# Strassen products for the first dense layer of the last stage, and an earlier place for the transposes of q and k

## The chip, the cores and the metric

The kernel runs on one core of one Trainium2 chip. The metric is the device time of one execution in microseconds (us): lower is better. The time before is the median of three runs.

## The reference, cut to what matters

```python
# chunked attention: 4 batches, 8 heads, 576 positions in chunks of 64, head size 64
attn = softmax(q_c @ k_c.T / 8)            # within each chunk
x    = attn @ v_c                          # -> 2304 tokens x 512
# 8 experts on every token, weights P from a Sinkhorn iteration over x @ w_gate
out  = sum_e P[:, e] * (relu(x @ w1[e]) @ w2[e])      # 512 -> 1024 -> 512
# last stage, on the experts' output x (2304 x 512)
h    = x @ w_in                            # 512 -> 1024
solu = h * exp(h - max(h)) / (sum(exp(h - max(h))) + 1e-9)
ln   = (solu - mean(solu)) / sqrt(var(solu) + 1e-6) * g_ln
out  = ln @ w_out                          # 1024 -> 512
```

## The kernel before, in words

**Precision.** Each large product is three matmuls: an operand is split into a high part (a copy on ScalarE, ACT) and a low part (source minus high, one subtraction on VectorE, DVE, or GpSimd, POOL). The function `split` does both; its subtraction is on DVE unless POOL is named. PASSES3 gives high*high, high*low, low*high.

**Stages.** The attention stage takes one tile of 128 tokens per step in the loop `for s in range(NT + 6)` (NT is 18, L1118). A step works on several tiles: exponentials of tile s-3, values (`attn_pv`, L277) of s-6, transposes of probabilities (`attn_pt`, L262) of s-5, scores (`attn_qk`, L217) of s-2, and at its end `attn_t(s)` (L199): the transposes of q (even s) or k (odd s) for a pair of tiles, evacuated from PSUM by ACT (L204) and DVE (L206). Scores of tile t need q and k of pair t//2, so for even t the k of the step just before. Side work (splits of the experts' weights and of x) goes to ACT and POOL in each step. The experts follow in 96 units (NM); already there the seven Strassen products of PRODUCTS are used for w1 (L653) and in pairs of units for w2 (`l2s`, L847). During the units the weights of the last stage are turned into two float32 parts on DVE, ACT and POOL, one small step at a time (`prep`, `mlp_steps`), and kept in DRAM.

**Last stage, per tile t of 128 tokens.** `mlp_x` loads x. `mlp_a` splits it (ACT and DVE). `mlp_b` (L1005) makes h: 24 matmuls of 512 columns into two PSUM banks; then the row maximum `nm` (L1019, DVE) and the exponential (L1020, ACT). `mlp_n` is the norm: the product un = h*ex (L1025, DVE), sums and statistics, one power on POOL (L1036), and the scaling of un (L1038). `mlp_c` (L1050) transposes un on PE and splits it (ACT, DVE). `mlp_d` (L1062) is the second layer, 24 matmuls of 512 columns, and stores the result. In the loop at L1294 a step s issues: `mlp_a(s+1)`, `mlp_b(s)`, `mlp_c(s-1)`, `mlp_n(s)`, `mlp_d(s-2)`.

**Passage.** After the last unit the last pair of units still has 14 products `l2s(last, k)`, k = 0 to 13, each with a DVE addition into the accumulator; the first tile's `mlp_b(0)` stands after k = 7. Then `l2s_sums` makes seven additions on DVE, one in each of the steps s = 3 to 9. The weights of the first layer arrive in eight tiles of 512 KB (`load_in`, tag "six", 15 buffers): one is loaded when a buffer is spare and seven as the x tiles of the last unit come free.

**Order.** The program runs in the order in which it is written (`manual_schedule`): each engine, and SP's DMA queue, works through its instructions in that order and stops at the first whose inputs or buffers aren't ready. PSUM tiles: four single banks ("r") and two double banks ("d").

Of the kernel before, what the change touches and what calls it, by code (L numbers as in the profile page):

```python
# [44 lines left out]
def chunk_attention_sinkhorn_moe_solu_kernel(  # L45
# [855 lines left out]
    raw64 = {}  # L901

    def load_mlp(n):
        i, j = divmod(n, 8)
# [6 lines left out]

    def mlp_steps(n):
        i, j = divmod(n, 8)
# [4 lines left out]
        def one():  # L918
            s["lo"], s["hi"] = raw64[n][:, :, 0], raw64[n][:, :, 1]
            s["b"] = two([P, 512], U32, f"wb{n}")  # L920
            ts(out=s["b"], in0=s["hi"], scalar1=3, scalar2=0x3FFFFFF8,
               op0=ALU.logical_shift_left, op1=ALU.bitwise_and)
# [32 lines left out]
        def store():  # L955
            for s_ in range(2):
                nc.sync.dma_start(
                    out=kept[i, s_][:, j * 512:(j + 1) * 512], in_=s["p"][s_].bitcast(F32)
                )

        return [one, two_, three, round_, rounded, size, flush_, parts, store]
# [3 lines left out]
    def load_in(kk, s_):  # L965
        t = six([P, F], F32R, f"mi{kk}_{s_}")
        nc.sync.dma_start(out=t.bitcast(F32), in_=kept[0, s_][:, kk * F:(kk + 1) * F])
        m_in[kk, s_] = t

    def load_out(n0, n1):  # L970
        for n in range(n0, n1):
            f, s_ = divmod(n, 2)
            if n % 3 == 0:
# [3 lines left out]
                out=t[:, n % 3].bitcast(F32), in_=kept[1, s_][:, f * DM:(f + 1) * DM]  # L977
# [16 lines left out]
    def mlp_a(t):  # L994
        x = xa.pop(t)
        xm[t] = [wtile([P, KD, P], F32R, f"xm{t}_{i}") for i in range(2)]
        split(xm[t][0], xm[t][1], x)

    def mlp_b(t):
        x = xm.pop(t)  # L1000
        ph = bank2(f"mh{t}")
        for n in range(2):
            for kk in range(KD):
                for i, (a, c) in enumerate(PASSES3):
                    nc.tensor.matmul(  # L1005
                        ph[:, n * 512:(n + 1) * 512],
                        x[a][:, kk, :],
                        m_in[kk, c][:, n * 512:(n + 1) * 512],
                        start=(kk == 0 and i == 0),
                        stop=(kk == KD - 1 and i == 2),  # L1010
                    )
# [64 lines left out]
    with tc.manual_schedule():  # L1076
# [41 lines left out]
        for s in range(NT + 6):  # L1118
# [33 lines left out]
            if s < NT:  # L1152
# [48 lines left out]
        for n in range(NM):  # L1201
# [30 lines left out]
            if n == NM - 1:  # L1232
                for t in range(3):
                    mlp_x(t)
            apart = n < 4
            parts = [(j, d, i) for d in (0, 2) for j in range(2) for i in range(2)]
            for i in range(7):
# [9 lines left out]
                if n == NM - 1:  # L1247
                    load_in(*divmod(i, 2))
# [90 lines left out]
```

## Time and profile before

| what | value |
|---|---|
| median of 3 runs | 1763.87 us (1761.92 to 1766.05) |
| profiled execution | 1770.89 us, its span 1769.1 us |
| busy share of the span | PE 99%, DVE 77%, POOL 62%, ACT 35% |
| attention stage | 0 to about 107 us |
| experts | about 107 to 1535 us |
| passage and last stage | 1534.7 us to the end |

Busy time of PE is the time in which a matmul is in flight; because matmuls overlap, the distance between the starts of groups tells more than their durations. A row names the line of the kernel, the engine, the operation, the tile written and the tiles read.

### The profile page before, as it was taken

The page shows a single profiled execution, that of the slowest core. Times are in us where ns is not written, and L with a number is a line of the kernel's source. Part 1 is how long each engine was busy: PE and PEld are TensorE (multiplying, and loading weights), DVE is VectorE, ACT ScalarE, POOL GpSimd, SP SyncE. Part 2 cuts the span into 40 slices and gives each one's busy share as a digit, 9 for nine tenths or more (in the row PEclk, how much of TensorE's full clock was granted, in tenths as well). Part 3 has the DMA queues.
Part 4 walks back from the last instruction along what each step waited for, and adds up shares of the span by engine and source line. Part 5 has one row for each costly group of instructions (what it writes and reads, how often), then busy time and mean ns, then how long its engine had stood idle before and what let it go on. Part 6 is the DMA issues. An engine that isn't in the chain of part 4 may idle for free. (4 is left out here: it accounts for less than half of the span.)

```text
span 1769.1 us, 32047 instructions
## 1 busy us (share of the span) xinstructions
PE 1744.6 (99%) x10809; PEld 1690.9 (96%) x10809; DVE 1364.3 (77%) x2249; ACT 627.2 (35%) x1424; POOL 1094.3 (62%) x1203
## 2 busy tenths in 40 slices
PE   8999999999999999999999999999999999999999
PEld 7899999999999999999999999999999999988887
DVE  5868888889987778787777688878777777776664
ACT  5843444444444223333322222232323222222222
POOL 2767988888887367778777766666666565400000
PEclk8999999999999999999999999999999999999999
DMA  9667899999898999989989999888888888931210
GB/s 221 175 221 261 297 316 331 324 344 325 317 332 322 342 340 339 332 293 357 313 295 343 337 329 369 302 284 281 283 264 281 276 276 253 311 110 49 66 49 30
DMA packets 299203, 481.45 MB, mean 272 GB/s; under 512 B 47248, under 2 KB 99616, under 8 KB 299040
## 3 DMA queue, kind: packets, MB, share of 16 engines
q1 hardware_dynamic: 298320, 475.47, 78.9%
q10 hardware_dynamic: 720, 3.93, 0.5%
q8 instruction: 87, 1.43, 0.3%
q14 instruction: 76, 0.62, 0.1%
HBM read 332.94 MB, written 146.35 MB: 271 GB/s over the span
## 5 line engine op out<-in xcount | busy, mean ns | idle before, releaser
L673 POOL TENSOR_TENSOR ho_T<-hT,ho_T 128x384 fp32r<-128x384 f32 x252 | 275.6, 1095 | 195.7 <-ACT ho_T L672 178.1
L796 PE MATMUL y<-h,w_A 128*128 128x384 f32 x1536 | 303.6, 335 | 0.5 <-DVE acc L823 0.5
L796 PEld LDWEIGHTS y<-h,w_A 128*128 128x128 f32 x1536 | 269.2, 188 | 1.3 <-ACT w_S L599 1.1
L672 ACT ACTIVATE ho_B<-hp 128x384 fp32r<-128x384 f32 x192 | 101.0, 526 | 416.7 <-DVE hp L706 400.2
L847 PE MATMUL y<-ho_T,wl_S 128*128 128x384 f32 x1152 | 231.4, 335 | 2.1 <-DMA wl_S<-wk 2.0
L152 POOL TENSOR_TENSOR w_A<-raw,w_A 128x256 fp32r<-128x256 f32 x224 | 173.1, 786 | 82.3 <-ACT w_A L151 77.9
L867 DVE TENSOR_TENSOR acc<-y,acc 128x768 f32<-128x768 f32 (+1 forms) x217 | 199.9, 923 | 24.3 <-PE y L847 24.0
L751 DVE TENSOR_TENSOR t<-Y,s 128x384 f32<-128x384 f32 x192 | 106.1, 553 | 136.8 <-PE Y L653 97.9
L847 PEld LDWEIGHTS y<-ho_T,wl_S 128*128 128x128 f32 x1152 | 202.7, 188 | 3.6 <-issue 2.6
L681 POOL TENSOR_TENSOR hT<-hp,hp 128x384 f32<-128x384 f32 x126 | 133.6, 1081 | 98.7 <-DVE hp L706 88.2
L672 ACT ACTIVATE ho_T<-hT 128x384 fp32r<-128x384 f32 x256 | 131.6, 516 | 125.2 <-POOL hT L681 120.5
L653 PE MATMUL X<-x_B,wl_A 128*128 128x384 f32 x768 | 154.6, 335 | 0.0
L653 PE MATMUL Y<-x_T,wl_S 128*128 128x384 f32 x768 | 154.1, 335 | 0.4 <-DVE t L751 0.3
L847 PE MATMUL y<-ho_B,wl_A 128*128 128x384 f32 x768 | 153.6, 334 | 0.3 <-DMA wl_A<-wk 0.3
L673 DVE TENSOR_TENSOR ho_B<-hp,ho_B 128x384 fp32r<-128x384 f32 x192 | 143.5, 747 | 3.9 <-ACT ho_B L672 3.3
L681 POOL TENSOR_TENSOR hT<-hp,hT 128x384 f32<-128x384 f32 x126 | 143.5, 1139 | 0.0
L1036 POOL TENSOR_TENSOR r<-r,mhalf 128x1 f32<-128x1 f32 x18 | 9.9, 550 | 208.8 <-DVE r L1033 208.8
L653 PEld LDWEIGHTS Y<-x_T,wl_S 128*128 128x128 f32 x768 | 134.7, 188 | 1.3 <-DVE t L751 1.3
L653 PEld LDWEIGHTS X<-x_B,wl_A 128*128 128x128 f32 x768 | 135.8, 189 | 0.0
L847 PEld LDWEIGHTS y<-ho_B,wl_A 128*128 128x128 f32 x768 | 134.7, 188 | 1.0 <-issue 1.0
L823 DVE TENSOR_TENSOR acc<-y,acc 128x768 f32<-128x768 f32 (+1 forms) x132 | 118.9, 901 | 5.0 <-PE y L796 4.5
L152 POOL TENSOR_TENSOR w_S<-ws,w_S 128x256 fp32r<-128x256 f32 x128 | 103.0, 822 | 6.3 <-ACT w_S L151 6.3
(169 smaller groups left out, 3463.1 us busy)
## 6 DMA issues: line engine op xcount, KB each, us to landing
wl_S<-wk SPq DMA_DIRECT2D x512, 256.0 KB, 4.8
wl_A<-wk SPq DMA_DIRECT2D x384, 256.0 KB, 4.7
wk<-w_S SPq DMA_DIRECT2D x256, 256.0 KB, 3.7
wk<-w_A SPq DMA_DIRECT2D x192, 256.0 KB, 3.4
raw<-in_moe_w_dram SPq DMA_DIRECT2D x71, 512.0 KB, 6.0
sh<-spread SPq DMA_DIRECT2D x64, 192.0 KB, 5.6
kept<-wp SPq DMA_DIRECT2D x32, 256.0 KB, 4.4
xk_T<-x_T SPq DMA_DIRECT2D x8, 768.0 KB, 4.3
```

What stands on the lines that cost most here:

```text
L152: (eng or nc.vector).tensor_tensor(out=lo, in0=src, in1=hi.bitcast(F32), op=ALU.subtract)
L653: nc.tensor.matmul(b, w[:, a, kk, :], x[:, c, kk, :], start=(first and kk == 0 and n == 0), stop=(kk == 1 and n == 2), skip_group_check=no ...
L672: nc.scalar.activation(out=hi, in_=x, func=AF.Copy)
L673: f = lambda: eng.tensor_tensor(out=lo, in0=x, in1=hi.bitcast(F32), op=ALU.subtract)
L681: eng.tensor_tensor(out=hb[m, n], in0=hb[m, a], in1=hb[m, b], op=ALU.subtract)
L751: nc.vector.tensor_tensor(out=c_of[n], in0=bank_, in1=c_of[other], op=ALU.add)
L796: nc.tensor.matmul(y, wo2[u, f"A{d // 2 + 1}{f + 1}"][:, a, i * P:(i + 1) * P], h[:, c, f, :], start=(f == 0 and n == 0), stop=(f == 1 and ...
L823: nc.vector.tensor_tensor(out=at, in0=y, in1=at, op=ALU.add)
L847: nc.tensor.matmul(y, wo2[unit(m + q_)[1], wn][:, a, i * P:(i + 1) * P], hop[m // 2, bn][:, q_, c, :], start=(q_ == 0 and o == 0), stop=(q ...
L867: nc.vector.tensor_tensor(out=at, in0=y, in1=at, op=ALU.add)
L1036: nc.gpsimd.tensor_tensor(out=r2, in0=r2, in1=mhalf, op=ALU.pow)
```

## The change

Part A, last stage. Two tiles are taken together as a pair r (tiles 2r and 2r+1), and their first layer is made of the seven Strassen products, each of six matmuls of 512 columns, 42 in place of 48. Sums of x are made by `mlp_s` (four on POOL) and split by `mlp_a` (four copies on ACT, four subtractions on POOL); `mlp_a` of pair r+1 is issued ahead of the norm of pair r. After the products ACT copies one bank and DVE makes five additions; `mlp_e` holds maximum and exponential, `mlp_m` the product un, `mlp_n` the rest of the norm. The weights' Strassen sums are prepared on POOL in `prep`, and 28 chunks of 256 KB are loaded in place of 16: three into buffers of tag "V", the others in tiles of up to 768 KB. The passage and the loop of the last stage are rewritten for pairs. Part B: from s = 3 `attn_t(s)` is the first work of its step.

```diff
-    kept = {}
-    for i in range(2):
-        for s_ in range(2):
-            kept[i, s_] = dram.tile([P, 4096], F32, name=f"kept{i}_{s_}")
+    kept_in = dram.tile([P, 28 * 512], F32, name="kept_in")
+    kept_out = [dram.tile([P, 4096], F32, name=f"kept_out{s_}") for s_ in range(2)]
+    M_IN = ("B11", "B12", "B22", "B21")
...
-        def parts():
+        def parts(n_=None):
+            f = s["b"].bitcast(F32) if n_ in (None, name) else carried[n_]
             s["p"] = [two([P, 512], F32R, f"wp{n}_{s_}") for s_ in range(2)]
-            split(*s["p"], s["b"].bitcast(F32), nc.gpsimd)
...
+        def less(to, a, b):
+
+            f = s["b"].bitcast(F32)
+            x = {"out": f, "in0": f, "in1": f}
+            for k, v in (("in0", a), ("in1", b)):
+                if v != name:
+                    x[k] = x["out"] = carried[v]
+            nc.gpsimd.tensor_tensor(op=ALU.subtract, **x)
+            carried[to] = x["out"]
...
+        put = lambda v: [lambda: parts(v), lambda: store(v)]
+        if name == "B11":
+            return steps[:-1] + [lambda: (flush_(), keep_b())] + put("B11")
+        if name == "B12":
+            return steps[:-1] + [
+                lambda: (flush_(), keep_b()), lambda: less("T1", "B12", "B11")
+            ] + put("T1")
+        if name == "B22":
+            return steps + put("B22") + [
+                lambda: (less("T3", "B22", "B12"), less("T2", "B22", "T1"))
+            ] + put("T3") + put("T2")
+        return steps + put("B21") + [lambda: less("T4", "B21", "T2")] + put("T4")
...
-    def load_in(kk, s_):
-        t = six([P, F], F32R, f"mi{kk}_{s_}")
-        nc.sync.dma_start(out=t.bitcast(F32), in_=kept[0, s_][:, kk * F:(kk + 1) * F])
-        m_in[kk, s_] = t
+    def load_in(n):
+
+        if n < 3:
+            t = vtile([P, 1, 512], F32R, f"mi{n}")
+            k0, k1 = n, n + 1
+        else:
+            t = six([P, 3, 512], F32R, f"mi{n}")
+            k0, k1 = 3 * n - 6, min(3 * n - 3, 28)
+        nc.sync.dma_start(
+            out=t[:, :k1 - k0].bitcast(F32).rearrange("p k x -> p (k x)"),
+            in_=kept_in[:, k0 * 512:k1 * 512],
+        )
+        for k in range(k0, k1):
+            x, r = divmod(k, 4)
+            m_in[XOPS[x], r // 2, r % 2] = t[:, k - k0]
 
...
-    def mlp_a(t):
-        x = xa.pop(t)
-        xm[t] = [wtile([P, KD, P], F32R, f"xm{t}_{i}") for i in range(2)]
-        split(xm[t][0], xm[t][1], x)
-
-    def mlp_b(t):
-        x = xm.pop(t)
-        ph = bank2(f"mh{t}")
-        for n in range(2):
-            for kk in range(KD):
-                for i, (a, c) in enumerate(PASSES3):
-                    nc.tensor.matmul(
-                        ph[:, n * 512:(n + 1) * 512],
-                        x[a][:, kk, :],
-                        m_in[kk, c][:, n * 512:(n + 1) * 512],
-                        start=(kk == 0 and i == 0),
-                        stop=(kk == KD - 1 and i == 2),
-                    )
+    xsum = {}
+
+    def mlp_s(r):
+
+        x0, x1 = xa[2 * r], xa[2 * r + 1]
+        ts = nc.gpsimd.tensor_tensor
+        s = xsum[r] = [two([P, 2, 2, P], F32, f"xs{r}_{i}") for i in range(2)]
+        ts(out=s[0][:, 0], in0=x1[:, 0:2], in1=x1[:, 2:4], op=ALU.add)
+        ts(out=s[0][:, 1], in0=s[0][:, 0], in1=x0[:, 0:2], op=ALU.subtract)
+        ts(out=s[1][:, 0], in0=x0[:, 0:2], in1=x1[:, 0:2], op=ALU.subtract)
+        ts(out=s[1][:, 1], in0=x0[:, 2:4], in1=s[0][:, 1], op=ALU.subtract)
+
+    def mlp_a(r):
+
+        x0, x1 = xa.pop(2 * r), xa.pop(2 * r + 1)
+        s = xsum.pop(r)
+
+        def put(n, src):
+            if n == "A22":
+                t = wtile([P, 2, 2, P], F32R, f"xm{r}_{n}")
+                p = [t[:, i] for i in range(2)]
+            else:
+                p = [wtile([P, 2, 2, P], F32R, f"xm{r}_{n}_{i}") for i in range(2)]
+            split(*p, src, nc.gpsimd)
+            return p
+
+        a = put("A1", x0.rearrange("p (h k) x -> p h k x", h=2))
+        for h in range(2):
+            xm[r, f"A1{h + 1}"] = [v[:, h] for v in a]
+        b = put("S12", s[0])
+        d = put("S34", s[1])
+        for i in range(2):
+            xm[r, f"S{i + 1}"] = [v[:, i] for v in b]
+            xm[r, f"S{i + 3}"] = [v[:, i] for v in d]
+        xm[r, "A22"] = put("A22", x1[:, 2:4])
+
+    mb = {}
+
+    def mlp_b(r, i):
+
+        if i == 0:
+            mb["r0"], mb["r1"] = bank2(f"mh{r}_0"), bank2(f"mh{r}_1")
+        r0, r1 = mb["r0"], mb["r1"]
+        at = {"X": r0[:, :512], "Z": r0[:, 512:], "Y": r1[:, :512]}
+        wn, xn, bn = PRODUCTS[i]
+        b, first = at[bn], i in (0, 1, 4)
+        x = xm.pop((r, wn))
+        for kk in range(2):
+            for n, (a, c) in enumerate(PASSES3):
+                nc.tensor.matmul(
+                    b, x[a][:, kk, :], m_in[xn, c, kk],
+                    start=(first and kk == 0 and n == 0),
+                    stop=(kk == 1 and n == 2),
+                    skip_group_check=not first,
+                )
+        if i == 0:
+            mb["s1"] = two([P, 512], F32, f"ms{r}")
+            nc.scalar.activation(out=mb["s1"], in_=b, func=AF.Copy)
+        elif i != 2:
+            to, other = {
+                1: ("t0", "s1"), 3: ("t1", "s1"), 4: (r1[:, 512:], "t1"),
+                5: (b, "s1"), 6: (b, "t0"),
+            }[i]
+            if i in (1, 3):
+                mb[to] = two([P, 512], F32, f"m{to}{r}")
+                to = mb[to]
+            nc.vector.tensor_tensor(out=to, in0=b, in1=mb[other], op=ALU.add)
+        if i == 5:
+            mlp_e(2 * r + 1, r1)
+        elif i == 6:
+            mlp_e(2 * r, r0)
+
+    def mlp_e(t, ph):
         ex = four([P, F], F32, f"ex{t}")
         un = four([P, F], F32, f"un{t}")
         nm = small.tile([P, 1], F32, tag="nm", name=f"nm{t}")
@@ -1020,9 +1132,12 @@
         nc.scalar.activation(out=ex, in_=ph, func=AF.Exp, bias=nm, scale=1.0, accum_out=su)
         stage[t] = (ph, ex, un, su, st, mv, r2)
 
+    def mlp_m(t):
+        ph, ex, un = stage[t][:3]
+        nc.vector.tensor_tensor(out=un, in0=ph, in1=ex, op=ALU.mult)
+
     def mlp_n(t):
         ph, ex, un, su, st, mv, r2 = stage.pop(t)
-        nc.vector.tensor_tensor(out=un, in0=ph, in1=ex, op=ALU.mult)
         nc.vector.tensor_scalar(out=su, in0=su, scalar1=EPS, scalar2=None, op0=ALU.add)
         nc.vector.reciprocal(out=su, in_=su)
         nc.vector.tensor_tensor(out=r2, in0=su, in1=su, op=ALU.mult)
@@ -1134,6 +1249,8 @@
             if s == NT:
                 a, b = w_steps(1), second_blocks(0)
                 w_side.extend(a[:4] + b[:2] + a[4:7] + b[2:] + a[7:])
+            if 3 <= s < NT:
+                attn_t(s)
             if 0 <= s - 3 < NT:
                 attn_exp(s - 3)
             if 0 <= s - 6 < NT:
@@ -1149,7 +1266,7 @@
                 attn_qk(s - 2)
             if 0 <= s - 3 < NT:
                 attn_norm(s - 3)
-            if s < NT:
+            if s < 3:
                 attn_t(s)
             run_side(3 if s >= NT + 3 else 2 if s >= NT else 1 + s % 2)
             if s >= 7:
@@ -1230,7 +1347,11 @@
                 for x in XOPS[:2]:
                     x_load(p + 1, x)
             if n == NM - 1:
+                assert not prep
                 for t in range(3):
+                    load_in(t)
+            if n == NM - 2:
+                for t in range(2):
                     mlp_x(t)
             apart = n < 4
             parts = [(j, d, i) for d in (0, 2) for j in range(2) for i in range(2)]
@@ -1245,7 +1366,11 @@
                     elif i < 5:
                         x_load(p + 1, XOPS[2 + i], nc.scalar)
                 if n == NM - 1:
-                    load_in(*divmod(i, 2))
+                    load_in(3 + i)
+                    if i == 3:
+                        mlp_s(0)
+                    if i == 5:
+                        mlp_a(0)
                 if n != NU - 1 or i > 2:
                     run_w(2 if i < 4 or n == 0 else 1)
                 if n:
@@ -1271,41 +1396,65 @@
                     l2s(n - 2 - n % 2, n % 2 * 7 + i)
             run_w(len(w_side))
         last = NM - 2
-        load_in(3, 1)
-        mlp_x(3)
-        mlp_a(0)
-        mlp_a(1)
         g = 7 * NM
+        sums = deque(l2s_sums(NPASS - 1))
         for k in range(14):
             for f in events.pop(g + k, ()):
                 f()
             l2s(last, k, apart=True)
+            if k in (2, 5):
+                load_in(10 + k // 3)
             if k == 7:
-                mlp_b(0)
-                mlp_a(2)
+                for i in range(7):
+                    mlp_b(0, i)
+                mlp_a(1)
+                mlp_m(1)
+                mlp_m(0)
+            if k == 1:
+                mlp_x(2)
+                mlp_x(3)
+            if k == 6:
+                mlp_s(1)
+            if k in (5, 10, 12):
+                sums.popleft()()
+        sums.popleft()()
         assert not events
-        load_out(0, 15)
+        load_out(0, 16)
+        mlp_n(1)
         mlp_n(0)
-        load_out(15, 16)
-        mlp_b(1)
-        mlp_n(1)
-        mlp_c(0)
-        sums = deque(l2s_sums(NPASS - 1))
-        for s in range(2, NT):
-            if s > 2 and sums:
+        mlp_x(4)
+        mlp_x(5)
+        NR = NT // 2
+        for r in range(1, NR + 1):
+            t1, t0 = 2 * r - 1, 2 * r - 2
+            if sums:
                 sums.popleft()()
-            if s + 2 < NT:
-                mlp_x(s + 2)
-            if s + 1 < NT:
-                mlp_a(s + 1)
-            mlp_b(s)
-            mlp_c(s - 1)
-            mlp_n(s)
-            mlp_d(s - 2)
-        mlp_d(NT - 2, 0, 6)
-        mlp_c(NT - 1)
-        mlp_d(NT - 2, 6)
-        mlp_d(NT - 1)
+            if r + 1 < NR:
+                mlp_s(r + 1)
+            if r + 2 < NR:
+                mlp_x(2 * r + 4)
+                mlp_x(2 * r + 5)
+            if 1 < r:
+                mlp_c(t1)
+            if r < NR:
+                for i in range(3):
+                    mlp_b(r, i)
+            if 1 < r:
+                mlp_c(t0)
+            if r < NR:
+                for i in range(3, 7):
+                    mlp_b(r, i)
+            if r + 1 < NR:
+                mlp_a(r + 1)
+            if r == 1:
+                mlp_c(t1)
+                mlp_c(t0)
+            if r < NR:
+                for f in (mlp_m, mlp_n):
+                    f(2 * r + 1)
+                    f(2 * r)
+            mlp_d(t1)
+            mlp_d(t0)
```

## Rows read from the trace of the kernel before

**Rows 1.** The page, its first part: busy time, share of the span, instructions of each engine.

```profile
PE 1744.6 (99%) x10809; PEld 1690.9 (96%) x10809; DVE 1364.3 (77%) x2249; ACT 627.2 (35%) x1424; POOL 1094.3 (62%) x1203
```

**Rows 2.** Stretches: start:end, length, then PE, PEld, DVE, ACT, POOL busy, clock, DMA.

```profile
60.00:85.00 25.00, 23.05 (x459) 20.74 (x459) 18.94 (x39) 21.40 (x45) 22.22 (x19) 1.00 0.77 208
...
1530.00:1545.00 15.00, 14.17 (x78) 13.03 (x77) 14.33 (x27) 4.96 (x10) 2.33 (x2) 1.00 1.02 367
...
1571.00:1769.00 198.00, 194.47 (x924) 161.96 (x922) 122.55 (x233) 54.04 (x98) 8.80 (x16) 1.00 0.15 50
```

**Rows 3.** Waits of PE over the span: line, releaser, total us, times, longest.

```profile
PE s L217 <- DVE kt L206: 7.0, 11, 1.8
```

**Rows 4.** Timeline of an even step: start, us, engine, line, instruction [idle before it].

```profile
47.60 0.44 PE L217 MATMUL s<-kt,qt 64*64 64x64 f32 x4 [0.45 <-DVE kt L206]
48.33 1.14 PE L217 MATMUL s<-kt,qt 64*64 64x64 f32 x28 [0.29 <-DVE kt L206]
```

**Rows 5.** Stretches of two microseconds in the attention stage.

```profile
10.00:12.00 2.00, 1.86 (x30) 1.68 (x30) 0.38 (x1) 0.00 (x0) 0.00 (x0) 0.50 1.16 206
...
30.00:32.00 2.00, 2.00 (x25) 1.88 (x22) 1.72 (x4) 0.28 (x2) 0.00 (x0) 0.58 1.15 290
```

**Rows 6.** Timeline of the last stage, PE, then one tile on ACT and DVE.

```profile
1670.98 5.61 PE L1005 MATMUL mh<-mi,xm 128*128 128x512 f32 x24
...
1676.43 1.04 PE L1050 MATMUL lt<-ident,un 128*128 128x128 f32 x8
...
1677.22 5.73 PE L1062 MATMUL po<-mo,lnt 128*128 128x512 f32 x24
...
1682.79 5.61 PE L1005 MATMUL mh<-mi,xm 128*128 128x512 f32 x24
...
1689.76 1.12 ACT L1020 ACTIVATE ex<-mh,nm 128x1024 f32<-128x1024 f32 x1 [5.65 <-DVE nm L1019]
...
1692.69 1.22 DVE L1025 TENSOR_TENSOR un<-mh,ex 128x1024 f32<-128x1024 f32 x1
...
1696.91 0.81 DVE L1038 TENSOR_SCALAR un<-un,mv,r 128x1024 f32<-128x1024 f32 x1
```

**Rows 7.** Lines by form: busy us, mean ns, then idle before and its releaser.

```profile
L152 DVE TENSOR_TENSOR lnt<-lt,lnt 128x512 fp32r<-128x512 f32 x36 | 23.2, 686 | 31.4 <-ACT lnt L151 31.4
...
L1019 DVE TENSOR_REDUCE nm<-mh 128x1 f32<-128x1024 f32 x18 | 22.0, 1225 | 26.8 <-PE mh L1005 26.8
...
L151 ACT ACTIVATE xm<-xa 128x512 fp32r<-128x512 f32 x18 | 11.1, 623 | 0.0
...
L152 POOL TENSOR_TENSOR wp<-wb,wp 128x512 fp32r<-128x512 f32 x16 | 20.8, 1303 | 17.1 <-ACT wp L151 17.0
...
L152 POOL TENSOR_TENSOR w_S<-ws,w_S 128x256 fp32r<-128x256 f32 x128 | 103.0, 822 | 6.3 <-ACT w_S L151 6.3
...
L867 DVE TENSOR_TENSOR acc<-y,acc 128x384 f32<-128x384 f32 x14 | 7.2, 548 | 0.5 <-PE y L847 0.5
...
L875 DVE TENSOR_TENSOR acc<-acc,acc 128x768 f32<-128x768 f32 x14 | 14.5, 1032 | 0.0
```

**Rows 8.** Timeline of the passage from the experts to the last stage, PE.

```profile
1542.50 2.48 PE L847 MATMUL y<-ho_T,wl_S 128*128 128x384 f32 x12 [0.25 <-DMA wl_S<-wk]
...
1554.73 2.06 PEld L847 LDWEIGHTS y<-ho_T,wl_A 128*128 128x128 f32 x12 [0.40 <-DVE acc L867]
...
1570.31 1.06 PE L1050 MATMUL lt<-ident,un 128*128 128x128 f32 x8 [0.98 <-DVE un L1038]
```

**Rows 9.** DMA issues of 1510 to 1560: operation, count, KB each, us to landing.

```profile
mi<-kept SPq DMA_DIRECT2D x8, 512.0 KB, 6.1
...
wl_S<-wk SPq DMA_DIRECT2D x13, 256.0 KB, 6.8
```

**Rows 10.** Line L673 on DVE: count, duration in ns minimum, median, maximum, first and last start.

```profile
L673 DVE TENSOR_TENSOR ho_B<-hp,ho_B x192: 541/559/1411, 603.7 to 1534.3; 128x384 fp32r<-128x384 f32 x192
L673 DVE TENSOR_TENSOR ho_T<-hT,ho_T x4: 542/542/543, 1539.4 to 1543.1; 128x384 fp32r<-128x384 f32 x4
```

More of the change, by code (lines that the diff above doesn't have):

```diff
@@ L891, in chunk_attention_sinkhorn_moe_solu_kernel, with mlp_chunk @@
     }
-    kept = {}
-    for i in range(2):
-        for s_ in range(2):
-            kept[i, s_] = dram.tile([P, 4096], F32, name=f"kept{i}_{s_}")
+    kept_in = dram.tile([P, 28 * 512], F32, name="kept_in")
+    kept_out = [dram.tile([P, 4096], F32, name=f"kept_out{s_}") for s_ in range(2)]
+    M_IN = ("B11", "B12", "B22", "B21")
     raw64 = {}
+    def mlp_chunk(n):
+        i, j = divmod(n, 8)
+        if i == 0:
+            c, name = divmod(j, 4)
+            name = M_IN[name]
+            j = 2 * (2 * (int(name[1]) - 1) + c) + int(name[2]) - 1
+            return i, j, c, name
+        return i, j, 0, None
     def load_mlp(n):
-        i, j = divmod(n, 8)
+        i, j, _, _ = mlp_chunk(n)
         src, r0, c0 = (w_in, (j // 2) * P, (j % 2) * 512) if i == 0 else (w_out, j * P, 0)
@@ L910, in load_mlp @@
         )
+    carried = {}
     def mlp_steps(n):
-        i, j = divmod(n, 8)
+        i, j, c, name = mlp_chunk(n)
         s = {}
@@ L919, in one @@
             s["lo"], s["hi"] = raw64[n][:, :, 0], raw64[n][:, :, 1]
-            s["b"] = two([P, 512], U32, f"wb{n}")
+            new = vtile if name in ("B11", "B12") else two
+            s["b"] = new([P, 512], U32, f"wb{n}")
             ts(out=s["b"], in0=s["hi"], scalar1=3, scalar2=0x3FFFFFF8,
@@ L949, in flush_, with store @@
                 nc.scalar.activation(out=f, in_=f, func=AF.Copy, scale=g_sb[:, j:j + 1])
-        def parts():
+        def parts(n_=None):
+            f = s["b"].bitcast(F32) if n_ in (None, name) else carried[n_]
             s["p"] = [two([P, 512], F32R, f"wp{n}_{s_}") for s_ in range(2)]
-            split(*s["p"], s["b"].bitcast(F32), nc.gpsimd)
-        def store():
+            split(*s["p"], f, nc.gpsimd)
+        def store(n_=None):
             for s_ in range(2):
-                nc.sync.dma_start(
-                    out=kept[i, s_][:, j * 512:(j + 1) * 512], in_=s["p"][s_].bitcast(F32)
-                )
@@ L961, in mlp_steps @@
-        return [one, two_, three, round_, rounded, size, flush_, parts, store]
-    m_in, m_out = {}, {}
-    def load_in(kk, s_):
-        t = six([P, F], F32R, f"mi{kk}_{s_}")
-        nc.sync.dma_start(out=t.bitcast(F32), in_=kept[0, s_][:, kk * F:(kk + 1) * F])
-        m_in[kk, s_] = t
+                if i == 0:
+                    k = 4 * XOPS.index(n_) + 2 * s_ + c
+                    to = kept_in[:, k * 512:(k + 1) * 512]
+                else:
+                    to = kept_out[s_][:, j * 512:(j + 1) * 512]
@@ new lines, in store @@
+                nc.sync.dma_start(out=to, in_=s["p"][s_].bitcast(F32))
+        def less(to, a, b):
[6 more added lines that the diff above has]
+            carried[to] = x["out"]
+        steps = [one, two_, three, round_, rounded, size, flush_]
+        if i == 1:
+            return steps + [parts, store]
@@ L972, in load_out @@
             f, s_ = divmod(n, 2)
-            if n % 3 == 0:
+            if n == 15:
+                m_out["t"] = vtile([P, 1, DM], F32R, f"mo{n}")
+            elif n % 3 == 0:
                 m_out["t"] = six([P, 3, DM], F32R, f"mo{n}")
@@ L976, in load_out @@
             nc.sync.dma_start(
-                out=t[:, n % 3].bitcast(F32), in_=kept[1, s_][:, f * DM:(f + 1) * DM]
+                out=t[:, n % 3].bitcast(F32), in_=kept_out[s_][:, f * DM:(f + 1) * DM]
             )
@@ new lines, in mlp_s @@
+    def mlp_s(r):
[13 more added lines that the diff above has]
+                p = [t[:, i] for i in range(2)]
+            else:
+                p = [wtile([P, 2, 2, P], F32R, f"xm{r}_{n}_{i}") for i in range(2)]
[10 more added lines that the diff above has]
+        xm[r, "A22"] = put("A22", x1[:, 2:4])
```

5 lines of the change are left out of this document (4 added, 1 removed).

## Prediction

> **What bounds the kernel now.** The page first: PE is in flight for 99% of the span, no other engine above 77% [rows 1]. So a change pays either by taking matmuls away or by closing the 1%, and it costs whatever makes PE wait. The stretches come next [rows 2]: the last stage keeps PE at 194.5 of 198 us while DVE works 122.6 and POOL 8.8; the passage into it (1530 to 1545) has the DMA queues at a share of 1.02; in the attention stage PE shows 23.05 of 25 us, with POOL at 22.2. Then the waits of PE [rows 3]: the largest single one is the scores waiting for k's evacuation by DVE, 7.0 us in 11 places. An even step shows it twice, 0.45 and 0.29 us [rows 4]. Last the timeline of the last stage [rows 6]: a tile's groups start at 1670.98 (first layer), 1676.43 (transposes), 1677.22 (second layer), 1682.79 (next first layer). So 24 matmuls of 512 columns take 5.45 us, 0.227 each; transposes 0.79; second layer 5.57; a tile 11.81. PE is gapless there, and all else lies beside it.
>
> **Part A, what goes.** 18 tiles x 24 matmuls become 9 pairs x 42: 54 fewer, 54 x 0.227 = -12.2 us. A pair needs 42 x 0.227 + 2 x (0.79 + 5.57) = 22.25 us of PE in place of 23.6.
>
> **Part A, what a pair adds.** DVE: five additions of 512 columns out of PSUM; the nearest row is lnt's 0.69 [rows 7]; two subtractions of about the same length move from DVE to POOL. ACT: a bank copy and one and a half more splits (0.62 each). POOL: four sums of 256 columns (0.82) and subtractions of 3 x 1.30 + 0.8, together 8 us [rows 7]. All engines have room in 22 us; the question is the chain. In a pair, product 3 (counting from 0) accumulates in the bank that an addition on DVE must have read after product 1, and that addition stands in DVE's queue behind the whole norm of the pair before. Walk the loop from the end of product 5: release 0.2, addition 0.7, maximum 1.23, addition 0.7, maximum 1.23, two products un 2.5 = 6.6. The norm of the first tile now meets a new wait: its power stands on POOL behind four subtractions, which start after the second exponential (1.12 [rows 6]) at about 6.0 and end at 10.6; power and scaling end at 12.2. The second norm takes 1696.91 + 0.81 - 1692.69 - 1.22 = 3.8 [rows 6], giving 16.0; two lnt subtractions 17.3, addition 18.0, products 3 to 5 4.1: 22.1 us. That is under PE's 22.25 by 0.15, so in the bare count PE stays the bound, but every tenth that DVE or POOL loses is paid.
>
> **Ports.** Line L673 on DVE takes 542 ns each time where POOL is out of work, and 559 in the median, 1411 at most, beside POOL's subtractions [rows 10]. In the old last stage POOL was nearly empty; in the new one it works 8 us of each pair beside DVE's SBUF-only operations (squares, scaling, sums). I charge 0.5 us for six steady pairs, +3; bounds 0 and +12 (1.75 x 7, if each of the six such operations in a pair meets a subtraction of 1.30 or a sum of 0.82, with a third of it hidden).
>
> The Trainium skill, page "SBUF — State Buffer", section "SBUF: two separate sides", says that VectorE and GpSimd hold their shared port pair as an exclusive lock for a whole instruction, the loser fully blocked. By that rule the upper bound is the case to expect; the spread in rows 10 agrees with it, though its median of 559 says that most instructions meet nothing.
>
> **The passage: loads.** The 14 products after the last unit wait for weights loaded behind `load_in` on SP's one queue. Before, product k = 6 already waited 0.25 us for its weights [rows 8], landing 6.8 us after issue [rows 9], with DMA at 367 GB/s and full. Now seven tiles of 768 KB stand ahead of it in place of eight of 512 KB, less one x tile of 256 KB that moves behind: 1 MB more, 2.9 us at that rate; three more chunks of 256 KB go ahead at the start of the unit, where part of them fits. Against it, the split of two tiles leaves DVE (two of about 0.69 [rows 7] and their wait for ACT). I take +2.0; bounds -1.9 (loads hidden, DVE waits gone) and +4.3. POOL's three sums and four subtractions for pair 0 are due only 10 us later: nothing. `load_out` and x of pair 2 come later on SP, but are read some 30 us later: nothing.
>
> **The passage: filling the pipe.** Let T be the end of the first pair's seven products, placed after k = 7. DVE's queue from there: additions and maxima to T+2.7, two products un to T+5.1, six accumulator additions (0.55) to T+8.2, three sums (1.03) to T+11.2, two norms (3.8) to T+18.8, a fourth sum T+19.8, and only then the addition that product 3 of the second pair waits for, T+20.5. PE has in the meantime six products of six 384-column matmuls (three quarters of 0.227 each: 6.1 us) and three products of the second pair (4.1): it is out of work at T+10.2 and waits 10.3 us in two places (banks of k = 12, and product 3). Then the second pair ends at U. ACT's queue there: exponential to U+4.1, four copies of pair 2's operands to U+6.3, and only then the copies of pair 0's transposed norm; DVE's subtraction follows at U+7.3. PE's second layer could have started at U+1.6: 5.7 us more. Together 16.0. The old passage paid 0.40 and 0.98 and a little more [rows 8], about 1.8. Net +14.2; bounds +5 (half of DVE's queue overlaps better than I count) and +18.
>
> **Other terms.** One of the last sums falls into the loop that has 0.15 us of slack, and the last pair has no products to stand between its two transposes, so the second waits for its norm: +2.5 (+1 to +3). Waits of 9 and 6 us on PE may drop its clock to the 1.2 GHz level, as after far shorter gaps in the attention stage, where the granted clock is 0.50 at 10 to 12 and 0.58 at 30 to 32 [rows 5]; two microseconds at half speed cost one: +2 (0 to +6). The weights' sums add some 18 us to POOL over hundreds of us of the experts, where it is 62% busy over the span [rows 1]: 0, at most +1.
>
> **Part B.** Transposes at the head of a step let their evacuations finish a step earlier; of the 7.0 us of waits only what the first scores wait stays, in a step that keeps its order. What is late next: on ACT the evacuations (up to three copies of 512 columns) stand ahead of exponential, value copy and probability copy, so the values wait for a double bank that ACT empties later; and POOL, 22.2 of 25 us busy between 60 and 85 [rows 2], can't be hurried. No DMA is issued by the moved step; q and k buffers come free earlier for SP. I take -3.0; bounds +1 and -13.9, which is all waits plus the 6.9 us that stretches at the low clock lose there (the two of rows 5 and seven like them).
>
> **Sum.** -12.2 + 2.0 + 14.2 + 3.0 + 2.5 + 2.0 - 3.0 = +8.5 us. The profiled execution, 1770.89 us (span 1769.1), would become 1779.4; it lies 7.0 us above the median, so the median goes from 1763.9 to 1772.4, and I say 1772.
>
> **Rivals.**
> 1. *Ports bound the last stage.* Each pair takes 24.0 us instead of 22.7, DVE's loop sets the pace, and the clock falls in the fill: +9 for pairs, +2 for the fill, +2 for the clock on top of 8.5: about 1785. For: the 1411 ns of rows 10. Against: their median. 0.20.
> 2. *The fill costs no more than before* (the other side). If the two norms of the first pair run beside the second pair's products as the old tiles' did, PE waits 1.8 us, not 16: -14.2 + 8.5 = -5.7, 1758. For: the old loop had the same queues and lost 1 us. Against: the old second tile needed no DVE addition in the middle of its products. It is faster by over 0.2% as soon as fill waits stay under 4 us. 0.20.
> 3. *Attention gives back all.* The transposes ahead close PE's gaps, the clock holds at 2.4 GHz after 24 us: -13.9 in place of -3, 1761. For: low stretches follow gaps. Against: POOL and ACT are nearly full there, and the first 24 us are start-up. 0.17, within 0.2% by itself.
> My forecast, PE-bound pairs with a costly fill: 0.43, its own range 1767 to 1780.
>
> **Chances.** This kernel can't tell less than 0.2% (3.5 us) from no change. Faster 0.21 (rival 2 and a little of 3), same 0.16 (rival 3 and the low edge of mine), slower 0.63. Range 1754 to 1789: from below rival 2 to above rival 1; a little lies outside on either side.
>
> **What would show it.** The last stage's pair period: 22.3 (PE-bound), 22.7 (forecast) or 24 (ports), and DVE's scaling (0.81 in rows 6) longer than before beside POOL. A wait of some 9 us before product 3 of the second pair, released by DVE, and one of 5 to 6 us before the first second layer; without them rival 2 holds. Products k = 4 and 6 waiting for DMA by 1 to 4 us. The waits of rows 3 gone, with smaller ones before the values. I am wrong if PE passes from 1535 us into the last stage with under 5 us of waits.

## The result and the profile after

The changed kernel takes 1788.0 us (median of four, 1787.6 to 1789.9) for 1763.5 of the kernel before beside it: ratio 1.0131, 95% interval 1.0119 to 1.0143, or +23.1 us (21.0 to 25.2); the two medians as such lie 24.5 us apart. The forecast was 1772, +8.5. Its profiled execution took 1787.64 us, span 1785.9. Two executions of the kernel before (2133.7 and 9832.3 us) and one of the experiment e3 (3463.9 us), far slower than all others of the same kernels, stand in no ratio.

The rows that answer to [rows 2], columns as there (start:end, length, PE, PEld, DVE, ACT, POOL busy, clock, DMA):

```profile
1530.00:1545.00 15.00, 12.90 (x63) 10.82 (x62) 12.25 (x18) 2.69 (x5) 9.66 (x9) 1.00 0.95 336
1545.00:1571.00 26.00, 15.60 (x73) 13.03 (x72) 21.00 (x37) 4.88 (x9) 7.03 (x6) 0.88 0.31 105
1571.00:1785.00 214.00, 195.25 (x894) 158.31 (x892) 143.90 (x253) 65.14 (x121) 63.94 (x72) 0.97 0.16 52
```

With fewer matmuls (x894 for x924) PE is busy as long in the last stage as before, and that in 214 us instead of 198; between 1545 and 1571 it is without work for 10.4 us. The waits of PE from 1500 us on (line, releaser, total us, times, longest) name what it waits for:

```profile
PE mh L1100 <- DVE mt L1117: 11.6, 6, 8.2
PE mh L1100 <- DVE mh L1117: 7.1, 9, 0.8
PE po L1177 <- DVE lnt L152: 5.2, 1, 5.2
PE y L847 <- DVE acc L867: 2.4, 3, 1.4
PE lt L1165 <- DVE un L1153: 1.1, 1, 1.1
PE y L847 <- DMA wl_S<-wk: 1.1, 1, 1.1
```

The 8.2 us in the first and the 5.2 in the third are the two long waits that the forecast named. The second was not forecast: nine times, once in each pair, product 5 of the first layer waits for an addition. The fill as a timeline (start, us, engine, line, instruction, idle before it):

```profile
1555.70 2.35 PE L847 MATMUL y<-ho_T,wl_A 128*128 128x384 f32 x12 [1.36 <-DVE acc L867]
...
1568.82 0.95 DVE L875 TENSOR_TENSOR acc<-acc,acc 128x768 f32<-128x768 f32 x1
1569.68 0.68 DVE L1117 TENSOR_TENSOR mt<-mh,ms 128x512 f32<-128x512 f32 x1
1570.42 5.21 PE L1100 MATMUL mh<-mi,xm_S 128*128 128x512 f32 x12 [8.24 <-DVE mt L1117]
...
1583.15 0.62 ACT L151 ACTIVATE xm_A<-xa 128x512 fp32r<-128x512 f32 x1
...
1585.02 2.04 ACT L151 ACTIVATE lnt<-lt 128x512 fp32r<-128x512 f32 x4
...
1586.38 13.91 PE L1177 MATMUL po<-mo,lnt 128*128 128x512 f32 x48 [5.19 <-DVE lnt L152]
```

The queues stand as the forecast walked them: on DVE two norms and a sum ahead of the addition at 1569.68, on ACT the operands' copies ahead of `lnt`. Behind each wait PE is slow: twelve matmuls take 5.21 us here and 3.02 in the steady pair below, 48 take 13.91 and 11.05. The clock there (columns as above):

```profile
1570.00:1576.00 6.00, 5.21 (x12) 3.79 (x12) 1.39 (x3) 0.00 (x0) 0.00 (x0) 0.57 1.05 385
1586.00:1592.00 6.00, 5.62 (x13) 4.47 (x14) 5.93 (x11) 1.06 (x3) 2.28 (x3) 0.50 0.00 0
```

Last, one steady pair. It answers to [rows 6]:

```profile
1696.82 1.03 PE L1165 MATMUL lt<-ident,un 128*128 128x128 f32 x8
...
1699.30 0.73 POOL L1058 TENSOR_TENSOR xs<-xa 128x256 f32<-128x256 f32 x1
1699.36 0.68 DVE L1152 TENSOR_TENSOR r<-r,su 128x1 f32<-128x1 f32 x1 [0.67 <-POOL r L1151]
1700.08 1.31 DVE L1153 TENSOR_SCALAR un<-un,mv,r 128x1024 f32<-128x1024 f32 x1
1700.11 0.74 POOL L1059 TENSOR_TENSOR xs<-xs,xa 128x256 f32<-128x256 f32 x1
...
1700.80 1.19 POOL L1060 TENSOR_TENSOR xs<-xa,xa 128x256 f32<-128x256 f32 x1
...
1702.51 0.68 DVE L1117 TENSOR_TENSOR mt<-mh,ms 128x512 f32<-128x512 f32 x1
1703.24 3.02 PE L1100 MATMUL mh<-mi,xm_S 128*128 128x512 f32 x12 [0.40 <-DVE mt L1117]
...
1706.30 0.70 DVE L1117 TENSOR_TENSOR mh<-mh,mt 128x512 f32<-128x512 f32 x1 [0.67 <-PE mh L1100]
1707.05 1.66 PE L1100 MATMUL mh<-mi,xm_A 128*128 128x512 f32 x6 [0.79 <-DVE mh L1117]
...
1709.90 11.05 PE L1177 MATMUL po<-mo,lnt 128*128 128x512 f32 x48
...
1720.79 1.04 PE L1165 MATMUL lt<-ident,un 128*128 128x128 f32 x8
```

The pair takes 23.97 us; PE's own work is 22.25. Product 3 is some 0.65 us late (0.40 shown as idle), product 5 some 1.1 late (0.79 shown). Behind a wait the first product also takes longer: the next one starts 1.49 us after product 5 (1707.05 to 1708.54), for 1.36 where nothing waits. The addition at 1706.30 reads bank Z, which product 4 filled, and writes the second half of the double bank `r1`. Product 5 accumulates into Y, the first half of `r1`, and starts at its end.

### The profile page after: what moved, and what is told of

Same layout as the page of the kernel before. It is cut to its first block, busy times and chain, and to the rows that moved or that the text cites. A ratio compares the mean times of both kernels' runs of the same rounds, so it can differ in the third digit from the quotient of the medians.

```text
span 1785.9 us, 32209 instructions
## 1 busy us (share of the span) xinstructions
PE 1734.4 (97%) x10755; PEld 1676.6 (94%) x10755; DVE 1389.8 (78%) x2276; ACT 643.9 (36%) x1457; POOL 1186.5 (66%) x1289
## 4 chain that ended last, share of the span: by engine, by line
PE 77%; DVE 7%; issue 5%; POOL 4%; DMA 4%; ACT 2%; SPq 0%; POOLq 0%; ACTq 0%; DVEq 0%
PE y L847 22%; PE Y L653 15%; PE y L796 14%; PE Z L653 10%; PE X L653 10%; PE mh L1100 2%; PE po L1177 2%; DMA wl_A<-wk 2%; POOL xm_S L152 1%; DVE nm L1131 1%; DMA wl_S<-wk 1%; DVE mh L1117 1%; DMA k<-in_k_dram 1%; POOL ho_T L673 1%; POOL hT L681 1%
## 5 line engine op out<-in xcount | busy, mean ns | idle before, releaser
L673 POOL TENSOR_TENSOR ho_T<-hT,ho_T 128x384 fp32r<-128x384 f32 x252 | 279.4, 1111 | 180.6 <-ACT ho_T L672 155.5
L673 DVE TENSOR_TENSOR ho_B<-hp,ho_B 128x384 fp32r<-128x384 f32 x192 | 142.3, 741 | 4.5 <-ACT ho_B L672 3.9
L681 POOL TENSOR_TENSOR hT<-hp,hT 128x384 f32<-128x384 f32 x126 | 139.4, 1107 | 0.0
L1177 PE MATMUL po<-mo,lnt 128*128 128x512 f32 x432 | 102.4, 397 | 5.2 <-DVE lnt L152 5.2
```

The lines of the kernel that those rows point to most:

```text
L673: f = lambda: eng.tensor_tensor(out=lo, in0=x, in1=hi.bitcast(F32), op=ALU.subtract)
L681: eng.tensor_tensor(out=hb[m, n], in0=hb[m, a], in1=hb[m, b], op=ALU.subtract)
L1177: nc.tensor.matmul(po[t], lt[f // 4][a][:, f % 4, :], m_out[f, c], start=(f == 0 and i == 0), stop=(f == KF - 1 and i == 2),)
```

## Experiments

Lateness is counted from start to start. Times are compared by their ratio to the kernel before on the same chip; 0.001 is 1.76 us. Traces are also compared by the stretch from the start of the last first-layer group of the experts to the end, since executions differ ahead of it: 236.5 us in the kernel before, 260.0 in the changed one.

**Part B alone (e1), part A alone (e2).** e1 is the kernel before with the moved call, e2 the changed kernel with it back:

```diff
+            if 3 <= s < NT:
+                attn_t(s)
             if 0 <= s - 3 < NT:
                 attn_exp(s - 3)
...
-            if s < NT:
+            if s < 3:
                 attn_t(s)
```

> The kernel before with part B alone (transposes of q and k first in their step from the fourth step on). Theory 1: the 6.7 us that lie between the two profiles ahead of the first layer come from the start of the kernel before, whose profiled execution had a lowered clock at 10 to 23 and 29 to 33 us and lies 7 us over the timed median; part B itself is worth nothing: 1763 (1761.5 to 1765). Rival: part B is worth what the two profiles show, 3 to 7 us: 1756.5 to 1760.5.

> The changed kernel with the transposes put back at the end of their step, so part A alone. Theory 1: 1788 (1786.5 to 1789.5), with a profile whose start shows the lowered clock again or not, but a stretch from the units' end to the end of 257 to 259 us as in the changed kernel. Rival (part B is worth 3 to 7 us): 1791 to 1795.

e1: 0.9984 (0.9974 to 0.9994), 2.8 us faster. e2: 1.0149 (1.0135 to 1.0162), 26.3 us slower, which is 3.2 above the changed kernel. Part B is worth about 3 us, as the forecast had it, so the half of theory 1 that calls it worth nothing falls. (2.8 us is less than the 3.5 that the forecast set as the least to tell; the interval of e1 lies below 1 all the same.) The waits of PE in e1's first 110 us:

```profile
PE px L277 <- ACT sm L248: 1.9, 4, 0.6
PE s L217 <- DVE kt L206: 1.5, 2, 1.2
...
PE pqk L199 <- DVE kt L206: 1.3, 2, 0.7
PE pt L262 <- POOL p L254: 1.2, 1, 1.2
PE s L217 <- DVE sm L253: 1.1, 1, 1.1
```

The 7.0 us of [rows 3] have become 1.5, and some 5.5 us of new waits stand beside them: in all PE waits 9.1 us there, for 9.6 before. So the gain does not lie in the waits. What differs is the granted clock (the last but two of each row, the kernel before first, then e1):

```profile
0.00:110.00 110.00, 100.02 (x1588) 90.64 (x1589) 71.88 (x147) 73.75 (x152) 60.35 (x70) 0.94 0.78 205
0.00:110.00 110.00, 99.86 (x1612) 89.11 (x1613) 73.76 (x155) 76.17 (x161) 64.59 (x76) 0.98 0.81 215
```

Counted as the forecast counted its 6.9 us, by stretches of two microseconds from 6 to 110 us, the low clock costs 6.9 and 6.8 us in the two traces without part B and 0 to 8.5 (mean 2.9) in the ten with it. The timed executions agree: the mean granted clock is 0.9968 in the kernel before and 0.9986 in e1, and the difference, taken as a share of 1763 us, is 3.2 us (an estimate). The other half of theory 1, the lowered clock, so holds, and part B has a hand in it; by what is not shown, nor why executions of the same instructions differ. The last first-layer group of the experts starts at 1532.6 and 1533.1 in the two traces without part B, and at 1524.8 to 1531.1 (mean 1527.6) in the ten with it; the clock is only a part of that spread.

**Bank Y as a tile of its own (e3, e11).**

```diff
+        if i == 1:
+            mb["y"] = bank(f"my{r}")
...
-        at = {"X": r0[:, :512], "Z": r0[:, 512:], "Y": r1[:, :512]}
+        at = {"X": r0[:, :512], "Z": r0[:, 512:], "Y": mb.get("y")}
...
-                5: (b, "s1"), 6: (b, "t0"),
+                5: (r1[:, :512], "s1"), 6: (b, "t0"),
```

> The changed kernel with bank Y as a tile of its own, and the third block's addition writing its sum into the double bank, so that product 5 no longer shares a tile with the addition that product 4 feeds. Theory 2: the 0.79 us wait ahead of product 5 (1.11 us late) is on the loop that sets a pair's time; without it a pair takes 22.9 us for 24.0, seven pairs and the first product round give 7 to 8 us: 1780.5 (1779 to 1783). Rival: the loop over VectorE and GpSimd (norm, power behind four subtractions, slower while both run) sets the pair, and the wait comes back ahead of product 3: a pair stays at 23.6 to 24.0, 1786 to 1788.

> The run with bank Y as a tile of its own, once more for its trace. Theory: no product 5 waits for the addition that reads Z, product 3 still waits for its own (0.4 us shown, 0.7 late), a pair takes 22.9 us. Rival: the loop over VectorE and GpSimd fills up what is taken out, product 3 waits 1.1 us longer and a pair stays at 23.9 to 24.0.

e3: 1.0074 (1.0059 to 1.0088), 10.1 us less than the changed kernel. Its trace can't be read beside the others, so e11 is the same kernel once more (1780.6 us, one run; its stretch to the end is 250.5 us for 260.0). PE in a pair of e11:

```profile
1669.95 1.04 PE L1167 MATMUL lt<-ident,un 128*128 128x128 f32 x8
...
1676.39 1.66 PE L1102 MATMUL my<-mi,xm_S 128*128 128x512 f32 x6 [0.42 <-DVE mt L1119]
1677.88 1.52 PE L1102 MATMUL mh<-mi,xm_S 128*128 128x512 f32 x6
1679.24 1.52 PE L1102 MATMUL my<-mi,xm_A 128*128 128x512 f32 x6
...
1692.85 1.04 PE L1167 MATMUL lt<-ident,un 128*128 128x128 f32 x8
```

Product 5 (1679.24) follows product 4 at once, product 3 is late as before, and the pair takes 22.90 us. Theory 2 holds: the second wait came from one tile holding two banks, not from data that product 5 needs.

**Without GpSimd's sums (e7).** In `mlp_s`, from the third pair on:

```diff
-        s = xsum[r] = [two([P, 2, 2, P], F32, f"xs{r}_{i}") for i in range(2)]
...
+        if r < 2:
...
+        else:
+            xsum[r] = [x.rearrange("p (h k) x -> p h k x", h=2) for x in (x0, x1)]
```

> The changed kernel, but from the third pair on the four sums and differences of x blocks on GpSimd are left out: the operands are made from the blocks as they are (the first layer then computes something else; every other instruction stands). Theory (port): the small VectorE operation and the scaling that now take 0.68 and 1.31 us beside them go back to 0.16 and 0.81, product 3 is no longer late (0.67 us), a pair takes 23.3 to 23.4: 3 to 4.5 us less than the changed kernel, ratio 1.0105 to 1.0115. Rival: what makes VectorE late is the power behind GpSimd's four subtractions (2.03 us) and the sums cost nothing: 1.0125 to 1.0135.

1.0102 (1.0087 to 1.0118), 5.1 us less than the changed kernel; its stretch to the end is 255.0 us for 260.0. The rows of e7 that answer to the pair above:

```profile
1693.39 1.03 PE L1168 MATMUL lt<-ident,un 128*128 128x128 f32 x8
...
1695.91 0.16 DVE L1155 TENSOR_TENSOR r<-r,su 128x1 f32<-128x1 f32 x1 [0.66 <-POOL r L1154]
1696.11 0.81 DVE L1156 TENSOR_SCALAR un<-un,mv,r 128x1024 f32<-128x1024 f32 x1
...
1699.18 2.97 PE L1103 MATMUL mh<-mi,xm_S 128*128 128x512 f32 x12
...
1702.95 1.66 PE L1103 MATMUL mh<-mi,xm_A 128*128 128x512 f32 x6 [0.79 <-DVE mh L1120]
...
1715.39 0.16 DVE L1155 TENSOR_TENSOR r<-r,su 128x1 f32<-128x1 f32 x1 [2.02 <-POOL r L1154]
...
1716.69 0.49 PE L1168 MATMUL lt<-ident,un 128*128 128x128 f32 x3
```

0.68 and 1.31 us are 0.16 and 0.81 again, product 3 is on time, and the pair takes 23.30: 22.25 and the wait of product 5. The power still stands 2.02 us behind the subtractions, so the rival falls. What GpSimd's sums cost DVE is real, and it is the smaller part of the pair's loss.

**The fill (e4, e5).** Both take the two norms out from ahead of the second pair and put them between its products. In e4 they stand behind the third pair's sums on GpSimd; in e5 ahead of these, with the loads of x moved up. This is e5's edit, cut:

```diff
-        load_out(0, 16)
-        mlp_n(1)
-        mlp_n(0)
         mlp_x(4)
         mlp_x(5)
+        load_out(0, 16)
...
+            if r == 1:
+                mlp_b(1, 0)
+                mlp_b(1, 1)
+                mlp_n(1)
+                for i in range(2, 5):
+                    mlp_b(1, i)
+                mlp_c(1)
+                mlp_n(0)
+                mlp_b(1, 5)
+                mlp_b(1, 6)
+                mlp_d(1, 0, 4)
+                mlp_c(0)
+                mlp_d(1, 4)
...
```

> The changed kernel with the fill of the last stage in another order: the norm of the first pair no longer ahead of the second pair's first addition on VectorE, but after it and after its third one, and the first transposes ahead of products 5 and 6, so that their copies lie ahead of the exponentials and of the operands' copies on ScalarE. Theory 3: the waits of 8.2 and 5.2 us go, and with them the lowered clock behind each (5 us): 8 to 14 us less, 1777 (1774 to 1780). Rival: VectorE's chain of two norms sets the fill, the waits only move to the first transposes: 0 to 4 us less, 1784 to 1788.

> The changed kernel with the fill reordered once more. In the fill before it, the first norm's power stood on GpSimd behind the sums of the third pair, which waited 18.4 us for their blocks of x (landed at 1579.9). Now the loads of those blocks are issued ahead of the 16 loads of the second weights, the norms' powers stand ahead of those sums, the first tile's transposes lie ahead of products 5 and 6, and the second one's between the halves of the first output tile. Theory 3: the waits of 8.2 and 5.2 us were made by the order alone: 8 to 16 us less than the changed kernel, ratio to the kernel before 1.004 to 1.0085. Rival: VectorE's two norms and its additions set the fill: 1.011 to 1.014.

e4 missed on the wrong side: 1.0179 (1.0166 to 1.0192). Its rows:

```profile
1579.93 0.72 POOL L1058 TENSOR_TENSOR xs<-xa 128x256 f32<-128x256 f32 x1 [18.42 <-DMA xa<-ak]
...
1582.77 0.55 POOL L1151 TENSOR_TENSOR r<-r,mhalf 128x1 f32<-128x1 f32 x1
...
1584.52 1.94 PE L1165 MATMUL lt<-ident,un 128*128 128x128 f32 x8 [18.54 <-DVE un L1153]
```

The norm that was moved behind GpSimd's sums waited with them for x, 18.4 us. e5 mends that: 1.0094 (1.0081 to 1.0108), 6.5 us less than the changed kernel, short of the 8 that theory 3 asked for and outside what the rival allowed. The waits of 8.2 and 5.2 us are gone from its trace, the granted clock is 1.00 from 1553 to 1588, and from the end of the first pair's products to the first transposes in the third pair's round it takes 38.2 us (1553.4 to 1591.6) for 50.1. Part comes back:

```profile
1591.61 1.94 PE L1165 MATMUL lt<-ident,un 128*128 128x128 f32 x8 [3.32 <-DVE su L1141]
```

These transposes wait 3.3 us for their norm, and that round runs 2.2 us longer. To the end e5 takes 250.2 us for 260.0. So this order takes away a third to a half of what the fill lost: 6.5 us by the timed runs and 9.8 by the trace, of some 21 (16 of waits and 5 of clock). Whether the rest is DVE's chain or the order of what stands behind it, e5 alone does not show; e9 below takes these 3.3 us away too, by moving that norm ahead.

**All of it (e6, e8, e9, e10).** e6 is e3 with the splits of a pair's first transposes (now `mlp_cs`) behind the first addition, e8 is e5 and e6 together:

```diff
+                ct = mlp_c(t1, r < NR)
...
                     mlp_b(r, i)
+                    if i == 1 and r > 1:
+                        mlp_cs(t1, *ct)
```

e9 mends the waits left in e8. Besides the lines here, against e8, the first half of the splits goes back ahead of the addition, and the last pair's first output tile is split round its second transposes:

```diff
+        load_out(0, 6)
         mlp_x(4)
         mlp_x(5)
-        load_out(0, 16)
+        load_out(6, 16)
...
                 mlp_b(1, 6)
+                mlp_s(2)
                 mlp_d(1, 0, 4)
+                mlp_m(3)
                 mlp_c(0)
+                mlp_n(3)
                 mlp_d(1, 4)
...
+                    if i == 4:
+                        for _ in range(min(len(sums), r - 1)):
+                            sums.popleft()()
```

e10, against e9:

```diff
-            if k in (2, 5):
-                load_in(10 + k // 3)
+            if k in (4, 6):
+                load_in(8 + k // 2)
...
+            if k == 9:
+                load_out(0, 16)
+                mlp_x(4)
+                mlp_x(5)
+            if k == 10:
+                mlp_m(1)
+                mlp_m(0)
```

> The changed kernel with bank Y as a tile of its own (as in the run before that had only this), and the splits of the pair's first transposes issued behind the first addition instead of ahead of it, on VectorE and ScalarE. Theory 2: neither wait on the additions is left (ahead of product 3: 0.67 us late, ahead of product 5: 1.11 us), a pair takes TensorE's own 22.3 to 22.5 us for 24.0: 10.5 to 13 us less than the changed kernel, ratio to the kernel before 1.006 to 1.0075 and 1 to 4 us under the run with the own tile alone. Rival: the loop over VectorE and GpSimd sets the pair: the wait moves to the first transposes of the next pair (un), a pair at 22.9 to 23.5: no faster than the own tile alone (1.0074).

> The changed kernel with the fill of this set's first run, bank Y as a tile of its own and the splits behind the first addition. If the causes found are the causes and add up: 18 to 28 us less than the changed kernel, ratio to the kernel before 0.997 to 1.003. If they overlap (one loop takes what the other gives): 1.004 to 1.008.

> The run with all three changes, mended where its trace still shows waits: the first half of the pair's first splits back ahead of the first addition (the second transposes waited 0.33 us in each pair for that bank); the third pair's first norm ahead of its operands' splits on GpSimd (3.3 us and the clock behind it); the first six loads of the second weights ahead of those of x (1.1 us); the three sums left over behind product 4 of the second and third round (1.8 us); the last pair's first output tile split round the last transposes (1.1 us). If these waits are what is left: a pair at 22.3 us, 7 to 11 us less than that run, ratio to the kernel before 0.996 to 0.998. Rival: the loop over VectorE and GpSimd is the bound now, the waits come back in other places: 1.000 to 1.002.

> The reordered run with the passage mended too: the loads of the second weights and of the third pair's x issued behind the tenth product group of the passage (they stood behind the store of the last sum on SyncE's queue, which idled from 1543 to 1562; the product waited 2.2 us for them), the two products of exponential and logit behind the eleventh (the additions behind them held TensorE for 1.4 us), the last two loads of the first weights one and two groups later. If TensorE waits for just these: 3.5 to 6 us less than that run, ratio to the kernel before 0.9955 to 0.9975. Rival: what is hidden here comes back at the first norm (the first transposes already waited 0.87 us for it): 0.998 to 1.000.

e6: 1.0077 (1.0065 to 1.0090), no faster than e3. Product 3 is on time, but with Y in the ring of four banks the second transposes now wait for the splits that were put off:

```profile
1676.48 0.60 PE L1168 MATMUL lt<-ident,un 128*128 128x128 f32 x4
1677.40 0.63 PE L1168 MATMUL lt<-ident,un 128*128 128x128 f32 x4 [0.32 <-DVE lnt L152]
```

A pair takes 22.73. The rival's time came, by another mechanism than it named. e8: 1.0023 (1.0013 to 1.0034), 19.1 us less than the changed kernel: e5 and e6 add up (6.5 + 9.5 = 16.0; the rest lies within the intervals). e9: 0.9992 (0.9983 to 1.0001), level with the kernel before; a steady pair takes 22.3 us, with no wait in it:

```profile
1677.71 1.03 PE L1168 MATMUL lt<-ident,un 128*128 128x128 f32 x8
...
1700.02 1.04 PE L1168 MATMUL lt<-ident,un 128*128 128x128 f32 x8
```

The rest of the stage is not free of waits. From 1500 us on PE waits 8.3 us in e9, for 2.0 in the kernel before, and the two largest are for DMA, the second layer's weights and those of the passage:

```profile
PE po L1187 <- DMA mo<-kept_out: 2.4, 2, 2.2
PE y L847 <- DMA wl_S<-wk: 2.0, 1, 2.0
```

Behind the longest of either (2.2 and 2.0 us) the granted clock is 0.68 (1574.8 to 1580) and 0.62 (1535.5 to 1540). So the stretch to the end is 235.3 us, only 1.2 less than in the kernel before, where the count of matmuls gives 12.2.

e10 missed: 1.0002 (0.9993 to 1.0011). What it hid came back elsewhere: 2.5 us on `hT` in place of `wl_S`, 1.4 on the first addition, 4.1 on `un` in four places for 1.0 in two. The version that beats both kernels, if by 2.8 us, is the smallest, e1. In the best order that was tried (e9) part A with part B beside it is no faster than part B alone; what it would be without e9's remaining waits is not shown.

## Why the prediction was right in sign and wrong in size

- **Part A, what goes: right.** The page counts 10755 matmuls for 10809 [rows 1], and in e9's steady pairs, where nothing holds PE, a pair takes the 22.3 us that the count gave: 12.2 us over nine pairs.
- **The loop of a pair: the step that failed**, at "addition 18.0, products 3 to 5 4.1". It let product 5 start behind product 4; it is some 1.1 us late in all nine rounds, 10.0 us that the sum did not hold. e3 and e11 show the place by taking it away (10.1 us by time, 9.5 by the trace). The diff had it in plain sight: `at["Y"]` and the target `r1[:, 512:]` of the fifth product's addition are two halves of one tile.
- **Ports: right in kind, a little small.** +3.0 forecast; the trace shows five pairs that lose some 0.65 each, 3.3 us, and e7 5.1 in all, with the late sum's wait smaller too (0.29 for 1.79). The forecast's bound of +12 does not follow from its own words: six operations with a third of 0.82 to 1.30 us hidden lose 3.3 to 5.2 us a pair, not 1.75; the runs show neither. The Trainium skill, "SBUF — State Buffer", section "SBUF: two separate sides", has an exclusive lock there, the loser fully blocked. The 0.68 us operation at 1699.36 agrees: it ends 0.01 us behind GpSimd's 0.73 us sum. The scaling is less plain: it loses 0.50 beside a sum of 0.74, and the sum after that takes 1.19; which of them held the other, and how long, the trace does not show. The forecast's upper bound did not come: in a steady pair these two operations are the ones that the sums stretch.
- **Rival 1** named a pair's 24.0 us and nearly the time, but of the 1.7 us that a steady pair lies above PE's work its ports made 0.6 to 0.7, and product 5 the rest.
- **Passage, loads: right in size, half right in the waits.** +2.0 forecast; the first pair begins 13.4 us after the last first-layer group's start, for 12.2 before: +1.2. Product k = 4 waited for its DMA (1.05 us), k = 6 did not; k = 5 and 6 waited for DVE's additions instead (0.62 and 0.43).
- **Passage, fill: right.** 16.0 us of waits forecast, in three places; these measure 1.36 + 8.24 + 5.19 = 14.8. Product 5 of the second pair, which it did not hold, adds 1.11: 15.9. e5 shows that the two long waits were the order's, and that a third to a half of the fill's loss goes with them.
- **Clock: too small.** +2.0 forecast, bound 6. From the end of the first pair's products to 1600.1 the fill takes 50.1 us; PE's own 28.3 (six products of the passage 6.1, the pair's seven 9.5, two transposes 1.6, two second layers 11.1) and the 15.9 of waits leave 5.9. Of this 5.0 stand in the two slow groups (5.21 for 3.02 us, 13.91 for 11.05), at 0.57 and 0.50; the other 0.9 is not placed.
- **Late sum and last pair: right**, 1.3 and 1.1 us for 2.5. **Part B: right in size, not by its way.** 2.8 for 3.0. The forecast took it from the waits of [rows 3]; these have only moved (9.1 for 9.6 us in all), and the gain shows in the clock, which is the way of rival 3, where it stood at 6.9 us. That the number came out is luck.

The sum again, with what was measured: -12.2 + 1.2 + 14.1 (15.9 less the old 1.8) + 5.9 + 3.3 + 2.4 - 2.8, and 8.9 for the other eight waits of product 5: +20.8, against +23.1 (21.0 to 25.2). Without part B the terms give 23.6, and from the last first-layer group on the traces say 23.5; the 2.3 us that the sum lacks lie ahead of it and stay open. The weights' sums on GpSimd, put at 0 to +1, were not tried by themselves. Of the 12.3 us between this sum and the forecast, 8.9 are the unseen wait and 3.9 the clock.

## What to carry to other kernels

Where a new loop is within a fraction of a microsecond of its bound (0.15 us here), walk every instruction's releaser, and treat all writers and readers of a tile as one: here two banks allocated together were waited for together. The products saved 12.2 us of matmuls and lost more, because the additions between them stood behind long work in DVE's queue; and every move past a queue (e4's norm behind sums that wait for a load) has to be checked there too. Ahead of a rewrite that leaves an engine at its bound, the small reordering is worth timing by itself. And a term whose size comes out right is worth a second look: part B's did, with its waits hardly changed.

## What the runs showed of the hardware

PE waited 8.2 us and 5.2 us, at the full clock of 2.4 GHz before, and the six microseconds from the end of each wait on show a granted clock of 0.57 and 0.50, the level of 1.2 GHz for most of them, though PE was busy for 5.21 and 5.62 of the six. The two waits so cost some 5.0 us beyond their own 13.4. In e5, without the two waits, the clock is 1.00 from 1553 to 1588. The waits of under a microsecond in each steady pair cost no clock: from 1672.87 to 1744.84 the granted clock is 1.00. GpSimd's sums of 0.73 us stretched a DVE operation of 0.16 us to 0.68 and one of 0.81 to 1.31; without the sums (e7) both are back.
